# Two attention layers mixed by a gate: the last turns of a P @ V unit take their blocks from a table

## The chip, the cores and the metric

The kernel runs on one core of a Trainium2 chip. The metric is the device time of one execution in microseconds (us), as the median of several runs. A profiled execution is a run of its own, with its own time.

## The reference

Two attention layers read the same x (2048 tokens of 512 features, 32 heads of 16). Layer A is plain softmax attention over all 2048 keys. Layer B works in four segments of 512 tokens: causal softmax attention inside a segment, mixed by a learned gate per head with a linear memory of the segments before. The results are mixed by a gate per token.

```python
# A
p = softmax(einsum("bhqd,bhkd->bhqk", q, k) * scale); o = einsum("bhqk,bhkd->bhqd", p, v)
a = o.reshape(B, S, D) @ wo
# B, for each of 4 segments s
p = softmax(einsum(qs, ks) * scale + mask); a_dot = p @ vs
a_mem = (phi(qs) @ M) / (phi(qs) @ z + 1e-6)
o = g * a_mem + (1 - g) * a_dot;  M += phi(ks).T @ vs;  z += sum(phi(ks))
# together
g = sigmoid((x * gate_w).sum(-1)); return g * a + (1 - g) * b
```

## The kernel before

Everything is fp32 or split into two parts that together carry it. The first stage (to about 330 us) projects q, k and v of both layers to DRAM. The second stage, which this change touches, is a software pipeline in *slots*; the Python loop that writes the program decides its whole order, and every engine then follows its own list in that order.

A **unit** is one side (A or B), one group of four heads and one chunk of 512 queries. There are 32 units of each side, taken in turn, A and then B; only the last pair stands the other way round. An A unit has 64 slots, one for each head and block of 128 keys; a B unit has 10, since its mask leaves out blocks. So a pair of units has 74 slots. In each slot:

- `score_part` (L662): TensorE makes one score product `st` of 128 keys by 512 queries (L677), and ScalarE takes its exponential into a tile `p` (L697, L700). There are three PSUM banks for `st`.
- `max_part` (L213), for the slot 96 places further on: TensorE makes the product `sm` of 128 queries by 512 keys (L204), and VectorE reduces it to row maxima `pm` (L225 for A; for B L237, which also applies the causal mask, in pieces). There are four PSUM banks for `sm`, L605. The maxima are later put into q so that the scores come out with them subtracted.

The two products of a slot use different rows of the array, and the trace shows them start within some nanoseconds of each other.

After each third slot there is a **turn** (L948 on). In a turn, `some_values` (L712) takes ready *blocks* from `queue` and multiplies them with v into one PSUM bank `ops` (L733). A block is 128 keys of four heads for A; B's ten blocks are the pieces in `PIECES` (L709): four of one key block, three of the next, then one, then two. Neighbouring blocks that share v are done by one **run** of matmuls, up to four blocks wide; a run is 4 heads x 2 records in the trace, whatever its width (a group in the timeline named x8 is one run, x16 two). A turn ends with its unit: `some_values` returns when a unit's last block is done, ScalarE copies `ops` out (`oraw`, L737), and for most A units 12 matmuls of the output projection of an earlier chunk (`output`, L838) take the next three turns, four matmuls in each; no blocks are done in those turns.

How many blocks a turn may take is `MOST = 3`, or one more when `jam` says that the queue is long. For B, `left` is zero, so that one more is allowed whenever over six blocks wait:

```python
def jam(n):
    left = SLOTS["A"] - queue[0][2] if queue and queue[0][1][0] == "A" else 0
    return 64 * (len(queue) - LOW) > (HIGH - LOW) * left
```

In the last 96 slots (`wide`) there are no more maxima, and turns of up to eight blocks come every six slots; after the last slot likewise.

Of the kernel before, what the change touches and what calls it, by code (L numbers as in the profile page):

```python
# [32 lines left out]
SLOTS = {"A": 64, "B": 10}  # L33
# [3 lines left out]
MOST = 3  # L37
LOW, HIGH = 6, 14
# [8 lines left out]
def gated_mix(ctx, tc, x, xT, wqkv, a_wo, b_wq, b_wk, b_wv, b_wo, beta, gate_w, out):  # L47
# [61 lines left out]
    nS = len(slots)  # L109
# [103 lines left out]
    def max_part(m, bank):  # L213

        u, (r, i) = maxs[m]
        side, g, c = u
        if u not in pmt:
            pmt[u] = mp.tile([128, 4, 4] + [4] * (side == "A"), F32, tag="pm" + side, name="pm")
        pm = pmt[u]
        ps = bank()  # L220
        if side == "A":

            kc, s, h = i // 8, i % 8 // 2, 2 * r + i % 2
            max_product(ps, u, h, s, 0, CH, kt_[u, kc])
            nc.vector.tensor_reduce(pm[:, h, s, kc:kc + 1], ps, axis=AX.X, op=ALU.max)  # L225
            flush_rows()
        else:


            k = kt_[u, c]  # L230
            mine = [(2 * r + h, s, 128 * (s == 2) + 256 * (s == 1 and h), 128 * (s + 1))
                    for h, s in (((0, 0), (0, 2)), ((0, 1), (1, 1)), ((1, 0), (1, 2)), ((0, 3),), ((1, 3),))[i]]
            for h, s, n0, w in mine:
                max_product(ps, u, h, s, n0, w, k)
            flush_rows()
            for h, s, n0, w in mine:
                rows_left.append(lambda h=h, s=s, n0=n0, w=w: nc.vector.tensor_tensor_reduce(  # L237
                    out=tri["rest"][:, 0:w], in0=ps[:, n0:n0 + w], in1=tri["mask"][:, CH - w:], scale=-1.0, scalar=3.0e38,
                    op0=ALU.add, op1=ALU.min, accum_out=pm[:, h, s:s + 1]))
            rows_left.pop(0)()  # L240
        if m == last_max[u]:
            def finish():

                due = min(e for e in a_last if e >= last_max[u]) + LATE_T
                late.append((min(due, first[u] + LEAD - 12), u, finish_max(u)))
            todo.append((m + 1, finish))

    def run_todo(m):

        for e in [e for e in todo if e[0] <= m]:  # L250
            todo.remove(e)
            e[1]()

    def run_late(pool, tag, m):
        while us := [e for e in late if e[0] < m][:2]:
            for e in us:
                late.remove(e)
            transpose_max(us, pool, tag)
# [3 lines left out]
    def loads(m):  # L262

        m = min(m, len(maxs) - 1)
        while loaded[0] <= m:
            u, (r, i) = maxs[loaded[0]]
            if loaded[0] == first_max[u]:
                load_q(u)
            kc = u[2] if u[0] == "B" else i // 8
            if (u, kc) not in kt_:  # L270
                load_k(u, kc)
            loaded[0] += 1
# [384 lines left out]
    wide = range(nS - LEAD + 2, nS - 4)  # L657
    assert wide.start % (2 * BURST) == wide.stop % (2 * BURST) == 0

    queue = []  # L660
# [51 lines left out]
    def some_values(n, most):  # L712

        while queue and most and queue[0][0] <= n:
            _, u, i = queue.pop(0)
            most -= 1
            side, g, c = u
            w = 1
            while (queue and most and queue[0][0] <= n and queue[0][1] == u and (i + w) // 4 == i // 4
                   and (side == "A" or PIECES[i + w][0] == PIECES[i][0])):  # L720
                queue.pop(0)
                most -= 1
                w += 1
            p = pt_[u, i // 4]
            if side == "A":
                c0 = q0 = 128 * (i % 4)
                v = vt[u][:, i // 16, i // 4 % 4]
            else:
                b, c0, q0 = PIECES[i]
                v = vt[u][:, b]  # L730
            done = i + w == SLOTS[side]
            for h in range(4):
                nc.tensor.matmul(ops[32 * h:32 * h + 17, q0:q0 + 128 * w], v[:, 17 * h:17 * h + 17], p[:, h, c0:c0 + 128 * w],  # L733
                                 start=(i == 0), stop=done, tile_position=(0, 32 * h))
            if done:
                raw = ob.tile([128, CH], F32, tag="o", name="oraw")
                nc.scalar.copy(raw, ops)  # L737
                nc.sync.dma_start(od[side, c][4 * g:4 * g + 4].rearrange("h r t -> (h r) t"), raw)
                stored.add(u)
                if side == "B" and c and g % 2 == 0:  # L740
                    octet("M", g // 2, c, n + 4)
                if (side, g ^ 1, c) in stored and u != ("A", NG - 1, NCH - 1):
                    octet(side, g // 2, c, n + (20 if side == "B" and (g < 5 or c < last) else 8))
                if u in between:
                    shared.extend(output(*between[u]))
                return
# [113 lines left out]
    def output(c, b, pairs, then, ps=ops):  # L860

        ks = [(os, o, i) for os in pairs for o in os for i in range(2)]
        for k in ks:
            def f(n, k=k):
                os, o, i = k
                assert loaded_blocks[c, b, os] > len(blocks) - 2
                t = blocks[loaded_blocks[c, b, os] - 1][:, i, o % 2].unsqueeze(1)
                list(products(ps, t, 0, "AB"[i], o, k == ks[0], k == ks[-1]))[n]()
                if k == ks[-1] and n == 2:
                    then(ps, c, b)  # L870
            for n in range(3):
                yield lambda n=n, f=f: f(n)
# [54 lines left out]
    for (side, o), b in early + [(k, b) for k in closing[:-1] for b in range(4) if (k, b) not in early]:  # L927
        close(nS - 66 if ((side, o), b) in early else max(nS, end[side, 2 * o + 1, last] + 60), side, o, b)

    def jam(n):  # L930


        left = SLOTS["A"] - queue[0][2] if queue and queue[0][1][0] == "A" else 0
        return 64 * (len(queue) - LOW) > (HIGH - LOW) * left

    filled = [0]
    n = 0
    while n < nS or queue or beside or filled[0] < len(fill):
        for f in beside.pop(n, []):
            f()  # L940
        if n < nS:
            score_part(n)
        m = n + LEAD
        if m < nS:
            loads(m + PRE)

            max_part(m, lambda: banks[m % 4])
        run_todo(m)  # L948
        if n >= nS or n % (2 * BURST if n in wide else BURST) == (2 * BURST if n in wide else BURST) - 1:
            if shared:  # L950
                for _ in range(4):
                    shared.pop(0)()
            else:
                some_values(n, 8 if n >= nS or n in wide else MOST + jam(n))
            if n < 5:


                for i in range(4):
                    nc.tensor.matmul(ops[:, 128 * i:128 * i + 128], identf, identf, start=True, stop=True)
            if any(e[0] < m + 1 for e in late):  # L960
                run_late(st_ps, "st", m + 1)
            else:
                for _ in range(0 if n >= nS and queue else 4):
                    if filled[0] == len(fill) or fill[filled[0]][0] > n:
                        break
                    fill[filled[0]][1]()
                    filled[0] += 1
        n += 1
# [12 lines left out]
def build():  # L981
    import concourse.bacc as bacc
    nc = bacc.Bacc("TRN2", target_bir_lowering=False, num_devices=1)
    shapes = {"x": (S, D), "xT": (D, S), "wqkv": (D, 3 * D), "a_wo": (D, D), "b_wq": (D, D), "b_wk": (D, D),
              "b_wv": (D, D), "b_wo": (D, D), "beta": (H,), "gate_w": (D,)}
    args = [nc.dram_tensor(n, s, F32, kind="ExternalInput").ap() for n, s in shapes.items()]
    out = nc.dram_tensor("out", (S, D), F32, kind="ExternalOutput").ap()
    with tile.TileContext(nc) as tc:
        gated_mix(tc, *args, out)
    return nc  # L990
# [23 lines left out]
```

## Time and profile before

| | |
|---|---|
| median of 3 runs | 1809.33 us (1809.08 to 1810.16) |
| the profiled execution: its own time | 1810.57 us |
| its span | 1808.7 us |
| TensorE matmul busy in the span | 1795.2 us (99%) |
| VectorE busy | 1574.9 us (87%) |
| ScalarE busy | 1447.0 us (80%) |
| GpSimd busy | 604.2 us (33%) |
| granted TensorE clock | 1.00 throughout |

The span begins with the program's first instruction and ends with its last; the profiled execution's own time has 1.9 us around it. Busy TensorE time is modelled by the profile, with the ends of pipelined matmuls overlapping, so that 99% does not say that TensorE has no room.

### The profile page before, as it was taken

The page shows a single profiled execution, that of the slowest core. Times are in us where ns is not written, and L with a number is a line of the kernel's source. Part 1 is how long each engine was busy: PE and PEld are TensorE (multiplying, and loading weights), DVE is VectorE, ACT ScalarE, POOL GpSimd, SP SyncE. Part 2 cuts the span into 40 slices and gives each one's busy share as a digit, 9 for nine tenths or more (in the row PEclk, how much of TensorE's full clock was granted, in tenths as well). Part 3 has the DMA queues.
Part 4 walks back from the last instruction along what each step waited for, and adds up shares of the span by engine and source line. Part 5 has one row for each costly group of instructions (what it writes and reads, how often), then busy time and mean ns, then how long its engine had stood idle before and what let it go on. Part 6 is the DMA issues. An engine that isn't in the chain of part 4 may idle for free.

```text
span 1808.7 us, 41561 instructions
## 1 busy us (share of the span) xinstructions
PE 1795.2 (99%) x15409; PEld 943.9 (52%) x15409; DVE 1574.9 (87%) x3333; ACT 1447.0 (80%) x2766; POOL 604.2 (33%) x708
## 2 busy tenths in 40 slices
PE   9999999999999999999999999999999999999998
PEld 7887766544444444444444444444444444444444
DVE  4224677899999999999999999999999999999920
ACT  5445444788888888888888888888888888888894
POOL 3001222234141414343433434342534342525442
PEclk9999999999999999999999999999999999999999
DMA  6568645543434344545454545454544443444541
GB/s 222 199 221 267 218 166 178 167 125 109 119 109 119 109 119 121 143 126 144 126 143 126 142 124 143 125 145 111 143 125 142 122 141 120 143 123 128 155 146 61
DMA packets 140617, 258.46 MB, mean 143 GB/s; under 512 B 36184, under 2 KB 60280, under 8 KB 139904
## 3 DMA queue, kind: packets, MB, share of 16 engines
q1 hardware_dynamic: 138912, 254.15, 47.1%
q8 instruction: 123, 2.02, 0.5%
q0 software_dynamic: 1216, 1.14, 0.2%
q14 instruction: 78, 0.64, 0.1%
q10 hardware_dynamic: 288, 0.52, 0.1%
HBM read 171.25 MB, written 83.25 MB: 141 GB/s over the span
## 4 chain that ended last, share of the span: by engine, by line
PE 90%; DVE 3%; ACT 3%; DMA 2%; issue 1%; POOL 1%; SPq 0%; POOLq 0%; DVEq 0%; ACTq 0%
PE ops L733 32%; PE st L677 27%; PE sm L204 14%; PE pr L313 10%; PE ops L838 4%; DVE pm L225 2%; PE sm L838 2%; ACT p L700 1%; DMA raw<-xT 1%; POOL mn L373 1%; PE num L495 1%; DMA vs<-wqkv 1%; DMA qdB<-q 0%; DMA qdA<-q 0%; ACT full L368 0%
## 5 line engine op out<-in xcount | busy, mean ns | idle before, releaser
L700 ACT ACTIVATE p<-st 128x512 f32<-128x512 f32 x2261 | 1190.2, 602 | 155.9 <-PE sm L204 96.0
L225 DVE TENSOR_REDUCE pm<-sm 128x1 f32<-128x512 f32 x2048 | 1280.2, 683 | 12.7 <-PE sm L204 11.6
L204 PE MATMUL sm<-kA,qA 48*128 48x512 f32 x2048 | 678.0, 435 | 0.3 <-DVE pm L237 0.2
L677 PE MATMUL st<-qA,kA 50*128 50x512 f32 x2014 | 670.4, 433 | 0.8 <-ACT p L697 0.5
L733 PE MATMUL ops<-p,vA 128*17 128x384 f32 (+3 forms) x7376 | 559.5, 406 | 0.0
L677 PEld LDWEIGHTS st<-qA,kA 50*128 50x128 f32 x2014 | 329.9, 185 | 391.7 <-ACT p L700 345.4
L204 PEld LDWEIGHTS sm<-kA,qA 48*128 48x128 f32 x2048 | 328.4, 184 | 22.1 <-issue 7.1
L792 POOL TENSOR_TENSOR rcp<-rec,minus 128x32 f32<-128x32 f32 x43 | 234.3, 5448 | 119.2 <-DMA rec<-dend 82.8
L733 PEld LDWEIGHTS ops<-p,vA 128*17 128x17 f32 x7376 | 152.4, 96 | 220.8 <-issue 178.6
L237 DVE CUSTOM_DVE_ANT_0 rest<-sm,mask 128x128 f32<-128x128 f32 (+3 forms) x512 | 247.0, 482 | 2.4 <-PE sm L204 1.5
L681 POOL TENSOR_SCALAR_AFFINE_SELECT p<-p 128x512 f32<-128x512 f32 x128 | 79.5, 639 | 351.2 <-ACT p L700 337.9
L204 PE MATMUL sm<-kB,qB 48*128 48x128 f32 (+3 forms) x512 | 166.2, 385 | 0.0
L376 DVE TENSOR_TENSOR q<-full,q 128x512 fp32r<-128x512 f32 x64 | 44.4, 694 | 87.3 <-ACT q L369 87.2
L677 PE MATMUL st<-qB,kB 50*128 50x512 f32 (+1 forms) x495 | 115.7, 333 | 1.7 <-ACT p L700 1.4
L677 PEld LDWEIGHTS st<-qB,kB 50*128 50x128 f32 x495 | 72.4, 186 | 59.5 <-ACT p L700 51.7
L733 PE MATMUL ops<-p,vB 128*17 128x512 f32 (+3 forms) x1024 | 87.2, 437 | 0.1
L204 PEld LDWEIGHTS sm<-kB,qB 48*128 48x128 f32 x512 | 79.9, 184 | 0.0
L368 ACT COPY full<-pr 128x512 f32<-128x512 f32 x64 | 37.4, 584 | 51.1 <-PE pr L313 50.9
L373 POOL TENSOR_SCALAR mn<-full 128x512 f32<-128x512 f32 x24 | 35.8, 1490 | 101.7 <-ACT full L368 81.3
L186 POOL CAST ms<-pm 128x16 fp32r<-128x16 f32 x32 | 6.3, 198 | 175.3 <-DVE pm L237 175.3
L186 POOL CAST ms<-nm 128x16 fp32r<-128x16 f32 x32 | 6.7, 210 | 172.8 <-DVE nm L182 172.8
L313 PE MATMUL pr<-xh,wql 128*128 128x512 f32 x128 | 54.8, 428 | 1.0 <-ACT xh L426 0.7
(178 smaller groups left out, 1580.6 us busy)
## 6 DMA issues: line engine op xcount, KB each, us to landing
kA<-kdA SPq DMA_DIRECT2D x256, 128.0 KB
vA<-vdA SPq DMA_DIRECT2D x31, 544.0 KB
kA<-kdA SPq DMA_DIRECT2D x256, 64.0 KB
qdA<-q SPq DMA_DIRECT2D x32, 256.0 KB
kdA<-q SPq DMA_DIRECT2D x32, 256.0 KB
qdB<-q SPq DMA_DIRECT2D x32, 256.0 KB
qA<-qdA SPq DMA_DIRECT2D x64, 128.0 KB
kdB<-q SPq DMA_DIRECT2D x32, 256.0 KB
```

The lines of the kernel that those rows point to most:

```text
L204: nc.tensor.matmul(ps[:, n0:n0 + n], rows(qt[u][:, :, s * 128:(s + 1) * 128], h, 48), rows(k[:, :, k0:k0 + n], h, 48), start=True, stop=True)
L225: nc.vector.tensor_reduce(pm[:, h, s, kc:kc + 1], ps, axis=AX.X, op=ALU.max)
L237: rows_left.append(lambda h=h, s=s, n0=n0, w=w: nc.vector.tensor_tensor_reduce(out=tri["rest"][:, 0:w], in0=ps[:, n0:n0 + w], in1=tri["mas ...
L313: nc.tensor.matmul(ps, l(a, k), r(b, k), start=(n == 0), stop=(n == 11))
L373: nc.gpsimd.tensor_scalar_min(ph["mn"], full, 0.0)
L376: nc.vector.tensor_sub(q2, full, q1.bitcast(F32))
L677: nc.tensor.matmul(ps[:, n0:n0 + CH - q0], rows(k[:, :, b * 128:(b + 1) * 128], h, 50), rows(q[:, :, q0:], h, 50), start=True, stop=True)
L681: nc.gpsimd.affine_select(out=x, in_=x, pattern=[[0, 4], [1, 128]], base=0, channel_multiplier=-1, compare_op=ALU.is_ge, fill=0.0)
L700: nc.scalar.activation(p[:, h], ps, AF.Exp, scale=SCALE)
L733: nc.tensor.matmul(ops[32 * h:32 * h + 17, q0:q0 + 128 * w], v[:, 17 * h:17 * h + 17], p[:, h, c0:c0 + 128 * w], start=(i == 0), stop=done ...
L792: eng.tensor_tensor(r, rec, minus, op=ALU.pow)
L838: yield lambda i=i, x=x, w=w: nc.tensor.matmul(ps, t[:, b, x], wos[side][:, o, w], start=start and i == 0, stop=stop and i == 2)
```

## The change

Which number of blocks a turn takes is no longer three plus `jam`. A table by side gives it for certain numbers of blocks that are left of the unit at the head of the queue; where the table has no entry, the old rule holds.

```diff
-    def jam(n):
-        left = SLOTS["A"] - queue[0][2] if queue and queue[0][1][0] == "A" else 0
-        return 64 * (len(queue) - LOW) > (HIGH - LOW) * left
+    ends = {"A": {9: 3, 8: 4, 7: 3, 6: 3, 5: 5}, "B": {10: 3, 7: 3, 4: 4}}
+
+    def most():
+        if not queue:
+            return 0
+        side = queue[0][1][0]
+        left = SLOTS[side] - queue[0][2]
+        over = 64 * (len(queue) - LOW) > (HIGH - LOW) * (left if side == "A" else 0)
+        return ends[side].get(left, MOST + over)
...
-                some_values(n, 8 if n >= nS or n in wide else MOST + jam(n))
+                some_values(n, 8 if n >= nS or n in wide else most())
```

## The prediction

> **What bounds the kernel now.** I began with the page's busy times, then asked for the busy time of each engine in stretches of the long second stage, then for the groups of instructions kept apart by shape.
>
> ```profile
> span 1808.7 us, 41561 instructions
> ...
> PE 1795.2 (99%) x15409; PEld 943.9 (52%) x15409; DVE 1574.9 (87%) x3333; ACT 1447.0 (80%) x2766; POOL 604.2 (33%) x708
> ...
> 400.00:700.00 300.00, 298.38 (x2948) 143.35 (x2942) 300.00 (x653) 264.93 (x514) 89.15 (x111) 1.00 0.38 110
> 700.00:1000.00 300.00, 300.00 (x2892) 140.95 (x2890) 299.00 (x635) 264.52 (x511) 115.25 (x132) 1.00 0.48 134
> ...
> L733 PEld LDWEIGHTS ops<-p,vA 128*17 128x17 f32 x7376 | 152.4, 96 | 220.8 <-issue 178.6
> L838 PE MATMUL ops<-woA,blk 128*128 128x512 f32 x132 | 46.0, 430 | 0.0
> ```
>
> In a row of a stretch the second figure is TensorE's busy time, the fourth VectorE's. Both look full, and only one can be the bound. From 400 to 700 us VectorE has not a hundredth of idle time; from 700 on, where output projections are worked in between units (132 matmuls of this kind at 6 a unit make 22 such units), it loses 1.0 us in 300. So in this stage the row maxima set the pace, and what a change of TensorE's turns can win is what VectorE still loses to TensorE. Idle time as the page counts it misses most of that, since a reduction of 0.68 us overlaps its follower. So I read VectorE's timeline at three neighbouring B units, all after an output projection.
>
> ```profile
> 877.93 4.34 DVE L225 TENSOR_REDUCE pm<-sm 128x1 f32<-128x512 f32 x7
> 882.19 0.68 DVE L237 CUSTOM_DVE_ANT_0 rest<-sm,mask 128x512 f32<-128x512 f32 x1
> ...
> 884.60 4.89 DVE L225 TENSOR_REDUCE pm<-sm 128x1 f32<-128x512 f32 x8
> 889.50 0.69 DVE L237 CUSTOM_DVE_ANT_0 rest<-sm,mask 128x512 f32<-128x512 f32 x1
> ```
> ```profile
> 922.22 4.48 DVE L225 TENSOR_REDUCE pm<-sm 128x1 f32<-128x512 f32 x7
> 926.70 0.69 DVE L237 CUSTOM_DVE_ANT_0 rest<-sm,mask 128x512 f32<-128x512 f32 x1
> ...
> 929.12 4.88 DVE L225 TENSOR_REDUCE pm<-sm 128x1 f32<-128x512 f32 x8
> 933.92 0.68 DVE L237 CUSTOM_DVE_ANT_0 rest<-sm,mask 128x512 f32<-128x512 f32 x1
> ```
> ```profile
> 831.02 4.48 DVE L225 TENSOR_REDUCE pm<-sm 128x1 f32<-128x512 f32 x7
> 835.50 0.69 DVE L237 CUSTOM_DVE_ANT_0 rest<-sm,mask 128x512 f32<-128x512 f32 x1
> ...
> 837.32 0.68 DVE L237 CUSTOM_DVE_ANT_0 rest<-sm,mask 128x512 f32<-128x512 f32 x1
> ...
> 837.93 5.00 DVE L225 TENSOR_REDUCE pm<-sm 128x1 f32<-128x512 f32 x8
> 842.85 0.68 DVE L237 CUSTOM_DVE_ANT_0 rest<-sm,mask 128x512 f32<-128x512 f32 x1
> ```
>
> Take the distance from a row's start to the next row's, by the number of reductions. The undisturbed price is the second pair of the second fence: 933.92 - 929.12 = 4.80 for 8, so 0.60 each. Against that the seven at 831.02 lose 4.48 - 4.20 = 0.28, those at 922.22 0.28, those at 877.93 0.06; the eight at 837.93 lose 4.92 - 4.80 = 0.12, those at 884.60 0.10. Since a pair of units is 74 slots, two more than 24 turns, the position of a unit against the turns repeats with every third pair: I take these three as the three kinds, seven of each, with one unit left over near the end of the stage.
>
> TensorE's timeline around the third kind says why:
>
> ```profile
> 831.16 0.50 PE L677 MATMUL st<-qA,kA 50*128 50x512 f32 x1
> ...
> 832.06 1.05 PE L733 MATMUL ops<-p,vB 128*17 128x512 f32 x8
> 833.04 0.50 PE L677 MATMUL st<-qA,kA 50*128 50x512 f32 x1
> ...
> 833.95 1.06 PE L733 MATMUL ops<-p,vB 128*17 128x384 f32 x16
> ...
> 834.94 0.50 PE L204 MATMUL sm<-kB,qB 48*128 48x512 f32 x1
> ...
> 835.84 0.62 PE L733 MATMUL ops<-p,vB 128*17 128x256 f32 x8
> ...
> 836.40 0.50 PE L204 MATMUL sm<-kB,qB 48*128 48x512 f32 x1
> ...
> 837.57 1.05 PE L733 MATMUL ops<-p,vA 128*17 128x512 f32 x8
> 838.56 0.49 PE L677 MATMUL st<-qA,kA 50*128 50x512 f32 x1
> ...
> 839.49 1.05 PE L733 MATMUL ops<-p,vA 128*17 128x512 f32 x8
> 840.47 0.50 PE L677 MATMUL st<-qA,kA 50*128 50x512 f32 x1
> ...
> 841.37 0.84 PE L733 MATMUL ops<-p,vA 128*17 128x384 f32 x8
> ...
> 842.15 0.50 PE L204 MATMUL sm<-kB,qB 48*128 48x512 f32 x1
> ```
>
> A turn lasts from its row to the next product: four blocks 832.06 to 833.04, 0.98; three blocks 841.37 to 842.15, 0.78; two blocks 835.84 to 836.40, 0.56. So a block is 0.21. A cycle (three products, one turn) takes 833.04 - 831.16 = 1.88 and 834.94 - 833.04 = 1.90 with four blocks, against 3 x 0.60 = 1.80 of VectorE: each turn of four in a row is 0.08 to 0.11 too long. How much VectorE has in stock is the time from a product's start to its own work on it: 835.50 - 834.94 = 0.56 is the shortest (the product itself is 0.50), 837.32 - 836.40 = 0.92 after the turn of two, so a stock of 0.36, and 842.85 - 842.15 = 0.70, a stock of 0.14.
>
> **The change part by part.** The built program's order of instructions shows what the table does. For A, nearly nothing: apart from the first unit, A's turns are as before, since `jam` makes the numbers left miss the table, and many A units still end with one block. For B, the turns of the ten blocks go from 4, 4 (a run of 3 and one of 1), 2 to 3, 3 (1 and 2), 4 (1, 1 and 2) wherever the queue holds them all, in the 22 units after output projections among others. They remain three turns, so each later turn, copy and DMA keeps its place in its queue (SP's, ScalarE's and GpSimd's lists have the same instructions in the same order), and the blocks are as many. The last 96 slots don't change.
>
> What is added is two more runs in a unit. A run's own price: 4 blocks in one run took 0.98 at 832.06, 3 and 1 took 834.94 - 833.95 = 0.99. So at most 0.01 a run, 0.02 a unit; I count it in.
>
> What moves: two times 0.21 leaves the first two turns, and 0.42 comes to the third. Stock of the third kind, step by step. At the product of 831.16 it is nil, since of the 0.28 lost from 831.02 on only 0.07 and 0.10 belong to the two cycles behind it, and the rest fell before. First turn of three: the cycle is 1.88 - 0.21 = 1.67, stock 0.13. Second: 1.90 - 0.21 + 0.01 = 1.70, stock 0.23. Both stalls are gone: the two cycles lost 0.07 and 0.10, 0.17 in all. Third turn, four blocks: 836.40 - 834.94 + 0.42 + 0.01 = 1.89, against VectorE's 837.32 - 835.50 = 1.82: stock 0.16. Before, the turn of two made a stock of 0.36 here; so that stock is lower, and the A turns that follow are the question.
>
> There a second effect answers. After the turn of two, the next cycle took 838.56 - 836.40 = 2.16, of which 837.57 - 836.40 = 1.17 went to the products instead of 833.95 - 833.04 = 0.91. These rows tell why, and what a closing turn of four does:
>
> ```profile
> 836.92 0.60 ACT L737 COPY oraw<-ops 128x512 f32<-128x512 f32 x1
> ```
> ```profile
> 868.79 1.05 PE L733 MATMUL ops<-p,vA 128*17 128x512 f32 x8
> ...
> 870.73 0.97 PE L838 MATMUL ops<-woA,blk 128*128 128x512 f32 x3
> ```
> ```profile
> 869.91 0.59 ACT L737 COPY oraw<-ops 128x512 f32<-128x512 f32 x1 [0.24 <-PE ops L733]
> ```
>
> The copy of `ops` ends at 837.52, and the next turn, which writes that bank, starts at 837.57: TensorE waited for it, 1.17 - 0.91 = 0.26. After a closing turn of four (an A unit's) the copy ends at 870.50, still ahead of the next user at 870.73, though it starts 1.12 after its turn does. That user came 870.73 - 868.79 = 1.94 after the turn's start, against 0.98 + 0.91 = 1.89 without any wait. So the copy is hidden by the longer turn and the products behind it, and the cycle is 0.91 to 0.96 + 0.98 = 1.89 to 1.94 instead of 2.16; if that cover failed, it would be the 0.26 again. Stock: 0.16 + 1.81 - 1.89 to 1.94 = 0.03 to 0.08, no stall. (VectorE's 1.81 is 837.93 - 837.32 plus two reductions.) The next turn of four: 1.80 - (840.47 - 838.56) = -0.11, so a stall of 0.03 to 0.08, I take 0.04, where 0.12 was. The third kind wins 0.17 + 0.08 = 0.25.
>
> First kind: 0.06 in B's turns, and the 0.10 at 884.60, for in its cycles the copy is hidden likewise:
>
> ```profile
> 882.46 0.84 PE L733 MATMUL ops<-p,vA 128*17 128x384 f32 x8
> 884.36 0.84 PE L733 MATMUL ops<-p,vA 128*17 128x128 f32 x16
> 886.05 1.06 PE L733 MATMUL ops<-p,vA 128*17 128x256 f32 x16
> ```
>
> Two turns of three, 1.90 and 1.69: the first holds 0.21 of ScalarE catching up with the copy, and a stock of 0.10 or more is left from it. Together 0.16. Second kind: 0.17 in B's turns as in the third; behind them it loses nothing before (the 4.80), and the stock of 0.03 to 0.08 lasts, as a turn of three follows. So three units win 0.25 + 0.16 + 0.17 = 0.58, seven times that is 4.1 us, and for the 22nd I count nothing. The ten other B units lie where VectorE loses nothing (400 to 700, and before), or in the last 96 slots: nothing. The span goes from 1808.7 to 1804.6. The profiled execution, 1810.57, is 1.2 above the median; from the median, 1809.33 - 4.1 = **1805.2 us**.
>
> A rule that speaks against the change: the Trainium skill, page "TensorE: Matmul & The Clock Gate", section "Wait — 56ns, not 53.3ns?", gives some 62 ns of sequencer time for each matmul where hardware decoding is off, which bounds short ones. By that the new third turn with its three runs, 24 records, would take 1.49 us as an estimate. The trace disagrees: the 16 records at 884.36 lie within 0.84 us, where the rule asks for 0.99.
>
> **The rivals.** *Short runs wait for weights.* Two runs of one block in a row stand nowhere in this program so far. The row of weight loads gives 96 ns each; were the four loads of a pass of one block done one after another and not hidden, the pass would take 0.38 instead of 0.10, a run with its two passes 0.56 more, the second turn 0.56 and the third 1.12 more. Less a stock of some 0.2 that is 1.5 us a unit, over 22 units +33, less the 4: 1838 us. It makes the kernel slower than now from some 0.4 a unit on. Against it: the turn of 1 and 2 at 884.36 has the 0.84 of the single run at 882.46. 5%. The rule of the Trainium skill that is weighed above would act in the same place, and milder.
>
> *The closing turn gives it back.* If the stock after the turn of four is nil, A's stalls of 0.12 and 0.10 stay and only B's go: 0.06 + 0.17 + 0.17 = 0.40, seven times 2.8, 1806.5 us. For it: my margin there is 0.03 to 0.08. 20%.
>
> *The copy is not hidden.* If the next cycle still takes 2.16, the stock there falls to 0.16 + 1.81 - 2.16 = -0.19: the second and third kind lose what they won, only the first gains, some 0.1: 1808.6 us. For it: ScalarE is busy 264.5 of 300 us from 700 on, and the copy stands in one list with the exponentials. Against it: 869.91. 10%.
>
> *More than forecast.* Every stall behind B's turns goes: 0.16 + 0.17 + 0.29 = 0.62, and some 0.2 for the 22nd: 1804.8 us; that lies inside the forecast's spread.
>
> **How the numbers follow.** The forecast has 65%. The range goes from 1804.2 (all stalls gone, and 0.6 of scatter, about half of what lies between the lowest and the highest of the three runs) to 1808.6 (the copy). What a measurement can tell from no change is about 0.2%, 3.6 us. Faster by more than that: most of the forecast (50 of 65) and a little of the second rival, 54%. Within it: the rest of the forecast, most of the second rival and the third, 41%. Slower by more: 5%.
>
> **What would show it.** In the changed profile, VectorE's rows behind the output projections run at 0.60 a reduction through B's three turns; the closing turn of four is 0.98 to 1.00 long; the next turn starts 1.9 after it and not after the copy; VectorE's busy time from 700 to 1000 us rises from 299.0 towards 299.5, and its last reductions come some 4 us earlier. I am wrong if B's third turn is over 1.2 long, if the stalls of 0.1 in the A turns behind it have grown, or if the next turn starts with the copy's end.

## The result, and the profile after

| | before | after |
|---|---|---|
| median of 13 runs | 1810.37 us | 1805.54 us |
| lowest to highest | 1808.81 to 1811.05 | 1803.96 to 1808.43 |
| span of the profiled execution | 1808.7 | 1804.1 |
| VectorE's first to last reduction of an A unit | 1537.5 | 1533.6 |

The ratio is 0.9977, with a 95% interval of 0.9968 to 0.9985: 2.7 to 5.8 us faster, where 4.1 were forecast. (It is taken over all the runs and is not that of the two medians, which would be 0.9973.) The last line of the table is the cleanest measure, since it leaves out the first 190 us and what their length differs by from one execution to the next. It comes from these rows, of the kernel before and after; the two times ahead of the semicolon are the first and the last start:

```profile
L225 DVE TENSOR_REDUCE pm<-sm x2048: 669/681/697, 192.1 to 1729.6; 128x1 f32<-128x512 f32 x187
```
```profile
L225 DVE TENSOR_REDUCE pm<-sm x2048: 669/679/694, 191.4 to 1725.0; 128x1 f32<-128x512 f32 x187
```

So 3.9 us were won between VectorE's first and last reduction, and 0.7 of the span's 4.6 had come before, in work that the change doesn't touch. I call this length VectorE's stretch below; each kernel's is from the same row of its own trace.

VectorE's timeline after, at units of the first, second and third kind:

```profile
876.51 4.27 DVE L225 TENSOR_REDUCE pm<-sm 128x1 f32<-128x512 f32 x7
880.70 0.68 DVE L237 CUSTOM_DVE_ANT_0 rest<-sm,mask 128x512 f32<-128x512 f32 x1
...
883.11 4.87 DVE L225 TENSOR_REDUCE pm<-sm 128x1 f32<-128x512 f32 x8
887.90 0.68 DVE L237 CUSTOM_DVE_ANT_0 rest<-sm,mask 128x512 f32<-128x512 f32 x1
```
```profile
920.59 4.38 DVE L225 TENSOR_REDUCE pm<-sm 128x1 f32<-128x512 f32 x7
924.89 0.68 DVE L237 CUSTOM_DVE_ANT_0 rest<-sm,mask 128x512 f32<-128x512 f32 x1
...
927.30 4.93 DVE L225 TENSOR_REDUCE pm<-sm 128x1 f32<-128x512 f32 x8
932.15 0.68 DVE L237 CUSTOM_DVE_ANT_0 rest<-sm,mask 128x512 f32<-128x512 f32 x1
```
```profile
829.77 4.39 DVE L225 TENSOR_REDUCE pm<-sm 128x1 f32<-128x512 f32 x7
834.08 0.68 DVE L237 CUSTOM_DVE_ANT_0 rest<-sm,mask 128x512 f32<-128x512 f32 x1
...
835.89 0.68 DVE L237 CUSTOM_DVE_ANT_0 rest<-sm,mask 128x512 f32<-128x512 f32 x1
...
836.50 5.03 DVE L225 TENSOR_REDUCE pm<-sm 128x1 f32<-128x512 f32 x8
841.44 0.68 DVE L237 CUSTOM_DVE_ANT_0 rest<-sm,mask 128x512 f32<-128x512 f32 x1
```

Read as before, at 0.60 a reduction: the seven lose 0 (880.70 - 876.51 = 4.19), 0.10 and 0.11, where they lost 0.06, 0.28 and 0.28; the eight lose 0, 0.05 and 0.14, where they lost 0.10, 0 and 0.12. B's turns gave what was forecast. What was to be seen behind them came true in the first kind and not in the third. The same stretch on TensorE, third kind:

```profile
829.91 0.50 PE L677 MATMUL st<-qA,kA 50*128 50x512 f32 x1
...
830.81 0.84 PE L733 MATMUL ops<-p,vB 128*17 128x384 f32 x8
831.58 0.52 PE L677 MATMUL st<-qA,kA 50*128 50x512 f32 x1
...
832.62 0.84 PE L733 MATMUL ops<-p,vB 128*17 128x128 f32 x16
...
833.40 0.50 PE L204 MATMUL sm<-kB,qB 48*128 48x512 f32 x1
...
834.30 1.06 PE L733 MATMUL ops<-p,vB 128*17 128x128 f32 x24
...
835.29 0.49 PE L204 MATMUL sm<-kB,qB 48*128 48x512 f32 x1
...
836.20 1.05 PE L733 MATMUL ops<-p,vA 128*17 128x512 f32 x8
837.18 0.50 PE L677 MATMUL st<-qA,kA 50*128 50x512 f32 x1
```

and on ScalarE:

```profile
830.08 0.59 ACT L878 COPY part<-ops 128x512 f32<-128x512 f32 x1
830.56 3.15 ACT L700 ACTIVATE p<-st 128x512 f32<-128x512 f32 x6
...
835.43 0.59 ACT L737 COPY oraw<-ops 128x512 f32<-128x512 f32 x1
```

B's turns are 0.77 (830.81 to 831.58), 0.78 and 0.99 long. The cycles, product to product, are 1.67, 1.82, 1.89 and 1.89. The copy of the finished unit ends at 836.02 and the next turn starts at 836.20: hidden. Of my cycles one is wrong, the second, forecast at 1.70. In it the products take 832.62 - 831.58 = 1.04 instead of 0.91. ScalarE says why: it had copied the output projection's result (`keep`, `part`) just before, and then ran six exponentials without a pause; TensorE's third score product of that cycle had to wait for a bank that was still being read. The weight load of that product shows the wait, and what ended it:

```profile
832.19 0.18 PEld L677 LDWEIGHTS st<-qA,kA 50*128 50x128 f32 x1 [0.30 <-ACT p L700]
```

The sign that I had named for the busy time hardly shows. VectorE is busy for 299.19 us from 700 to 1000, against 299.00 before and 299.5 looked for:

```profile
700.00:1000.00 300.00, 300.00 (x3006) 144.03 (x2995) 299.19 (x637) 265.75 (x514) 116.87 (x134) 1.00 0.50 133
```

What was won stands in the distances between starts, and only to a small part in the idle time.

### The profile page after: what moved, and what is told of

It reads as the page before. It is cut to its first block, busy times and chain, and to the rows that moved or that the text cites. A ratio compares the mean times of both kernels' runs of the same rounds, so it can differ in the third digit from the quotient of the medians.

```text
span 1804.1 us, 42457 instructions
## 1 busy us (share of the span) xinstructions
PE 1791.4 (99%) x15857; PEld 954.9 (53%) x15857; DVE 1571.3 (87%) x3333; ACT 1449.2 (80%) x2766; POOL 604.0 (33%) x708
## 4 chain that ended last, share of the span: by engine, by line
PE 91%; DVE 2%; ACT 2%; DMA 2%; POOL 1%; issue 1%; SPq 0%; POOLq 0%; ACTq 0%; DVEq 0%
PE ops L733 32%; PE st L677 27%; PE sm L204 14%; PE pr L313 10%; PE ops L838 4%; PE sm L838 2%; DVE pm L225 1%; ACT p L700 1%; POOL mn L373 1%; DMA raw<-xT 1%; PE num L495 1%; DMA qdA<-q 0%; DMA vs<-wqkv 0%; DMA qdB<-q 0%; DVE q L376 0%
## 5 line engine op out<-in xcount | busy, mean ns | idle before, releaser
L733 PE MATMUL ops<-p,vA 128*17 128x128 f32 (+3 forms) x7368 | 559.7, 407 | 0.0
L733 PEld LDWEIGHTS ops<-p,vA 128*17 128x17 f32 x7368 | 152.3, 96 | 223.7 <-issue 179.5
L733 PE MATMUL ops<-p,vB 128*17 128x128 f32 (+3 forms) x1480 | 88.1, 353 | 0.1
```

## The experiments

VectorE's stretch is 1537.5 before and 1533.6 after. Ratios are of a kernel's runs to those of the kernel before, with their intervals; they can't tell most of these kernels apart, the stretch and the rows can. Besides, I compared the 2048 starts of VectorE's reductions one by one with those of the kernel before, each counted from its own first: that tells where along the stretch time is won. A pair of units is taken from one B unit to the next, and a mean by kind is over the seven units of that kind.

**A's entries alone.**

```diff
-    ends = {"A": {9: 3, 8: 4, 7: 3, 6: 3, 5: 5}, "B": {10: 3, 7: 3, 4: 4}}
+    ends = {"A": {9: 3, 8: 4, 7: 3, 6: 3, 5: 5}, "B": {}}
```

> The table keeps its entries for A and loses those for B, so that B's turns are 4, 4, 2 again. Theory (the stock of row maxima that VectorE has in front of it decides, and only B's turns change it): the kernel before, within 0.5 us, and the losses of 0.28 and 0.12 in VectorE's rows around B's turns are back. Rival (A's entries bring a part): between the two kernels, 1 us or more faster than before.

Ratio 0.9998 (0.9988 to 1.0007); the stretch is 192.9 to 1730.4, 1537.5, as before, and pair by pair the starts agree with the kernel before within 0.06 us. So two executions of nearly the same order repeat that closely, and the whole effect is B's.

**Every run one block wide.**

```diff
-            while (queue and most and ...
+            while (False and queue and most and ...
```

> The changed kernel with every run of P @ V one block wide: turns and their sizes are as they are, 2368 runs instead of 1105. Theory (a run's own price is 0.005 to 0.01 us, since its weights are loaded behind the matmuls before it): turns of three and four get 0.01 to 0.03 longer, VectorE loses that where its stock is nil, 0 to 3 us slower than the changed kernel. Rival 1 (weights are not hidden: 0.56 a run): several hundred us slower. Rival 2 (sequencer time of 62 ns a matmul, the rule of the Trainium skill's page TensorE: Matmul & The Clock Gate as I used it): a turn of three takes 1.49 us, some 300 us slower.

Ratio 0.9995 (0.9985 to 1.0004); the stretch is 190.8 to 1725.9, 1535.1, so 1.5 more than the changed kernel for 1262 more runs (18944 matmul records on L733 against 8848, eight a run; the expectation's count is one higher). By the ratios it would be 3.3 more, with intervals that touch. All of the 1.5 comes behind the first output projection, at 733 us; ahead of it, where VectorE has stock, these runs cost nothing. A turn of three single runs, here the first row, x24, to the product behind it, takes 840.31 - 839.53 = 0.78, as with one run:

```profile
839.53 0.85 PE L733 MATMUL ops<-p,vA 128*17 128x128 f32 x24
840.31 0.50 PE L204 MATMUL sm<-kB,qB 48*128 48x512 f32 x1
```

Short runs are nearly free here; both rivals fall. By the rule of the Trainium skill's page "TensorE: Matmul & The Clock Gate" (section "Wait — 56ns, not 53.3ns?"), as I used it, 24 matmuls would have asked for 1.49 us, an estimate; the trace has 0.78. The page gives that rule for hardware decoding switched off, and no run here says which it was: the trace shows that this bound does not act here, not that the page is wrong.

**The other order in B: 4, 2, 4.**

```diff
+    ends = {"A": {}, "B": {10: 4, 6: 2, 4: 4}}
```

> B's turns are 4, 2, 4; nothing else differs from the changed kernel but A's entries of the table, which do nothing. Theory (the order inside the unit matters by the stock at each turn): the first turn loses its 0.07 again in the second and third kind, the turn of two fills the stock, the closing turn of four hides the copy, A's turns behind lose at most what they lose in the changed kernel: 2 to 3 us faster than before over the second stage. Rival 1 (all that matters is that the closing turn hides the copy): as the changed kernel, 3.9. Rival 2 (all that matters is that no two turns of four stand together inside B): 1.5 or less.

Ratio 0.9991 (0.9982 to 1.0000); the stretch is 190.8 to 1727.5, 1536.7: 0.8 less than before. But in this execution the granted clock fell once, at 423 to 427 us, well ahead of the first output projection. The row of that stretch (granted clock is the figure 0.77; VectorE is busy 4.61 of 6.00) and its neighbours:

```profile
400.00:424.00 24.00, 23.81 (x214) 11.10 (x206) 24.00 (x59) 21.17 (x42) 6.12 (x9) 0.99 0.16 47
424.00:430.00 6.00, 6.00 (x64) 2.79 (x64) 4.61 (x10) 4.34 (x9) 5.07 (x5) 0.77 0.46 139
430.00:460.00 30.00, 30.00 (x325) 14.82 (x323) 30.00 (x63) 26.41 (x52) 10.70 (x13) 1.00 0.44 120
```

VectorE is idle for 1.39 there, and its starts come 1.46 later from there on. Without that the stretch is 2.2 less than before: within the theory's 2 to 3, well off 3.9 and above 1.5. By kind the pairs win 0.19, 0.04 and 0.07, where the changed kernel wins 0.19, 0.17 and 0.17. So both the order inside B and the closing turn count.

**The closing copy cut short, in the kernel before.** Twice, since the first try had a flaw of its own:

```diff
 # first try
+                if side == "B":
+                    nc.gpsimd.memset(raw[:, 64:], 1.0)
+                    nc.scalar.copy(raw[:, :64], ops[:, :64])
...
 # second try: two fixed tiles, set once at the start
...
+                raw = oraws[len(stored) % 2]
+                cut = 64 if side == "B" else CH
+                nc.scalar.copy(raw[:, :cut], ops[:, :cut])
```

> The kernel before, but ScalarE's copy of a finished B unit takes 64 of 512 columns; the rest is set to one. Theory (after a closing turn of two TensorE waits 0.26 for that copy, and the losses of 0.12 and 0.10 in the A turns behind it come from that wait): the cycle behind it falls from 2.16 to 1.9, those losses go, the 0.17 in B's own turns stay; about 1.5 us faster than before. Rival (the A turns lose time because turns of four follow each other, whatever the copy does): before within 0.3 us.

The first try was slower, 1.0026 (1.0015 to 1.0037), stretch 190.3 to 1733.1, 5.3 longer. TensorE's list of waits has a row that stands in none of the others:

```profile
PE mt_ps L195 <- POOL ms L187: 4.6, 6, 1.2
```

TensorE waited six times, 4.6 us, for the maxima that GpSimd prepares for their transpose; the added memset stood in GpSimd's list. At the first of these waits it ran only at 791.74, behind a long division, so the unit was stored late; GpSimd's next division, which reads that unit back, started 20.4 us after the one before it instead of 17.3, and the maxima came behind that. Read for the question asked, this run is spoilt by its own edit.

> The kernel before once more with a short copy of a finished B unit (64 of 512 columns; the rest of the stored tile is old), this time without setting the rest on GpSimd in each unit: two fixed tiles are set once at the start. Theory: as the rows of the earlier attempt have it inside the units, where the A turns behind B lost 0.05 and nothing instead of 0.12 and 0.10, and B's own 0.17 stayed: about 1.1 us faster than before over the second stage, and no loss of 1 us anywhere. Rival (the short copy itself makes the kernel slower, as it came out then): 3 us or more slower than before.

The second try: 0.9992 (0.9983 to 1.0001), stretch 192.7 to 1728.4, 1535.7, so 1.8 shorter, where 1.1 was expected. VectorE's rows at a unit of the third kind:

```profile
831.21 4.47 DVE L225 TENSOR_REDUCE pm<-sm 128x1 f32<-128x512 f32 x7
835.69 0.69 DVE L237 CUSTOM_DVE_ANT_0 rest<-sm,mask 128x512 f32<-128x512 f32 x1
...
838.11 4.92 DVE L225 TENSOR_REDUCE pm<-sm 128x1 f32<-128x512 f32 x8
842.95 0.68 DVE L237 CUSTOM_DVE_ANT_0 rest<-sm,mask 128x512 f32<-128x512 f32 x1
```

The seven still lose 4.48 - 4.20 = 0.28, the eight 0.04 instead of 0.12. By kind the pairs win 0.13, 0.01 and 0.07. B's turns are as they were and A's loss goes with the copy alone: the two terms of the forecast are two effects, and this is the second by itself. Both rivals fall, that the short copy makes the kernel slower and that A's turns lose time whatever the copy does. Of the 0.7 beyond the 1.1 expected, 0.1 comes ahead of the first output projection and 0.1 in the 22nd pair, neither of which was counted, and the rest in the pairs, most of it in the first kind.

**The output projection's copy cut short, in the changed kernel.**

```diff
-        nc.scalar.copy(part[b], ps)
+        nc.gpsimd.memset(part[b][:, 64:], 0.0)
+        nc.scalar.copy(part[b][:, :64], ps[:, :64])
 # and the same in leave
```

> The changed kernel, but ScalarE's copies of the output projection's result (keep and leave) take 64 of 512 columns; the rest of the result is set to zero. In the changed profile the first of B's turns is followed by a cycle of 1.75 to 1.82 us instead of the 1.67 that I forecast, since the exponentials start late behind that copy. Theory (TensorE waits there for ScalarE, and that is why the third kind of unit still loses 0.05 and 0.09 in A's first turns): the cycle falls to about 1.68, those losses fall to 0.04 or less, 0.7 to 1.2 us faster than the changed kernel. Rival (the first cycle is long for another reason, or its stock would be lost anyway): the changed kernel within 0.3 us.

```profile
836.18 4.89 DVE L225 TENSOR_REDUCE pm<-sm 128x1 f32<-128x512 f32 x8
840.99 0.68 DVE L237 CUSTOM_DVE_ANT_0 rest<-sm,mask 128x512 f32<-128x512 f32 x1
```
```profile
830.51 0.84 PE L733 MATMUL ops<-p,vB 128*17 128x384 f32 x8
832.20 0.84 PE L733 MATMUL ops<-p,vB 128*17 128x128 f32 x16
```

B's first turn starts 1.69 before the second, where the changed kernel has 832.62 - 830.81 = 1.81, and the eight lose 4.81 - 4.80 = 0.01 instead of 0.14. Ratio 0.9976 (0.9965 to 0.9987); the stretch is 189.9 to 1723.8, 1533.9, 0.3 longer than the changed kernel's; but here too the granted clock fell once, to 0.57 from 374 to 378 us, and VectorE's starts come 1.2 later from there on. Behind it the kernel is 0.9 faster, which the theory gave, and the third kind wins most of that: 0.27 a pair instead of 0.17. So the misjudged cycle was ScalarE's doing.

**VectorE's work cut.** Row maxima over 448 of 512 columns.

```diff
-            nc.vector.tensor_reduce(pm[:, h, s, kc:kc + 1], ps, axis=AX.X, op=ALU.max)
+            nc.vector.tensor_reduce(pm[:, h, s, kc:kc + 1], ps[:, :448], axis=AX.X, op=ALU.max)
```

> The changed kernel, but VectorE's row maxima of A take 448 of 512 columns. Theory (VectorE sets the pace of the second stage and TensorE is close behind, with cycles of 1.68, 1.89 and 2.07 us): the pace passes to TensorE, 35 to 60 us faster, and VectorE no longer busy throughout; not the 64 x 0.067 = 4.3 us a pair, 120 us in all, that VectorE alone would give. Rival (TensorE sets the pace already): 5 us or less.

Ratio 0.9864 (0.9851 to 0.9878); the stretch is 191.2 to 1702.2, 1511.0: 22.6 shorter than the changed kernel's. That VectorE sets the pace holds. My 35 to 60 was too much: TensorE stands closer behind than I had added up, above all where the change acts. Of the 22.6, 15.3 are won by 733 us; behind the first output projection 7.3 are left, 0.34 a pair, though each pair's 64 reductions were made some 4 us shorter (0.615 instead of 0.679 each). From there on TensorE's products, which VectorE waits for, come hardly faster than VectorE had worked. As an estimate from this, some 7 us is all that an order of turns without a stall could still win there. Now it is VectorE that waits:

```profile
700.00:1000.00 300.00, 300.00 (x3004) 144.98 (x3001) 282.38 (x648) 268.22 (x518) 118.14 (x136) 1.00 0.46 130
```

**Two attempts at more.** What VectorE still loses lies mostly in the three turns of the output projection. In one kernel its matmuls take four turns of three (with one more buffer for `p`), in the other A's turns of four are spread:

```diff
 # four turns of three
-NP = 6
+NP = 7
-                for _ in range(4):
+                for _ in range(3):
 # A's turns spread, in most()
+        over = over and (prior[0] < 2 or len(queue) > 16)   # prior: turns of four just before
```

> The changed kernel with the twelve matmuls of an output projection in four turns of three instead of three turns of four, and one more buffer for p, since blocks wait longer. Most of what VectorE still loses (0.25 to 0.66 us a pair) lies in those three turns, whose cycles are 2.03 to 2.08 us. Theory (a cycle of 2.07 falls to about 1.86 and the stock holds): the losses there fall by two thirds, some 6 us; one turn fewer for blocks makes up to three more turns of four in a pair, which give back 0 to 5 us: 1 to 6 us faster than the changed kernel. Rival (what is taken from these turns comes back in full in the turns that catch up): within 1 us of it, or slower.

> The changed kernel, with the output projection in three turns of four as there, and A's turns of four spread: a turn of four may not follow two others while at most sixteen blocks wait. In the built program no three turns of four stand together any more in A's part of the stage shown. Theory (stock): the losses of the changed kernel in A's turns behind B (0.05 and 0.09 in the second and third kind) and further on go, those in the projection's turns (0.25 to 0.66 a pair) stay or fall where the turns ahead of them leave more stock: 1 to 2 us faster than the changed kernel (3.9 faster than before over the second stage). Rival: within 0.5 us.

Four turns of three: 0.9977 (0.9968 to 0.9986), stretch 191.2 to 1723.4, 1532.2. A's turns spread: 0.9975 (0.9965 to 0.9985), stretch 190.6 to 1723.0, 1532.4. Both are 1.2 to 1.4 shorter than the changed kernel's 1533.6, at the lower end of what was expected, and by their medians (1805.51 and 1805.32) not to be told from it. For the first, most of what the projection's turns no longer lose is lost again in the turns that catch up: against the changed kernel, three pairs win 1.3 in the first ten reductions from the projection on and lose 1.2 of it over the rest. What the seventh buffer does by itself was not run. Both together, with fours allowed early:

```diff
-LOW, HIGH = 6, 14
+LOW, HIGH = 0, 1
... # NP and the projection's turns of three as above
+        over = over and (prior[0] < 2 or len(queue) > 12)
```

> The output projection's matmuls again in four turns of three with seven buffers for p; besides, a turn of four may not follow two others while at most twelve blocks wait (LOW, HIGH = 0, 1, so that fours come early). Theory (with the projection's turns cut, what is left is lost where three and more turns of four stand together, and a turn of three gives 0.11 to the stock each time): 1 to 3 us faster over the second stage than the run with four turns of three alone (5.3 faster than before). Rival (fewer fours in a row here are more fours elsewhere, and the loss only moves): within 0.7 us of that run.

A miss: 1.0023 (1.0011 to 1.0036), stretch 190.2 to 1729.8, 2.1 longer than before. It loses already where no other order did (two executions lost there to their clock), ahead of the first output projection. From 335 to 700 us, this kernel first and the changed one below:

```profile
335.00:700.00 365.00, 362.30 (x3390) 158.43 (x3394) 364.59 (x794) 316.63 (x621) 105.81 (x136) 1.00 0.39 113
```
```profile
335.00:700.00 365.00, 362.67 (x3684) 176.19 (x3680) 365.00 (x799) 322.85 (x625) 106.03 (x136) 1.00 0.40 115
```

By its built order the turns there go 4, 4, 3, 4, 4, 3, 2, 4, 3, 4, 1, 3 and so on: fours come early, and turns of one and two follow them. As I read it, these short turns come when the stock can take no more; no run shows that by itself. I had only thought of fours standing together. The rows show 0.4 of idle time and five operations fewer; by the starts, this kernel is 3.2 us behind the kernel before when the first output projection comes. Behind that point it wins 1.2, where four turns of three alone win 5.1. So its early fours cost 3.2, and its later turns give up 3.9 more of what it was to win. Part of its ratio is something else again: see the granted clock below.

## Why the prediction was right, and where it wasn't

- *VectorE sets the pace, and the change is worth what VectorE stops losing*: shown, by the run with lighter reductions and by the rows; but from 733 us on even the lighter reductions shorten a pair by only 0.34 us, so there TensorE stands close behind.
- *A's entries do nothing*: shown.
- *A run costs at most 0.01*: held; the turn of 1, 1 and 2 is 0.99 long, and 1262 more runs cost 1.5 us of the stretch in all.
- *B's own turns win 0.06, 0.17 and 0.17*: the rows have 0.06, 0.18 and 0.17.
- *The closing turn of four hides the copy*: held, at 836.02 against 836.20; the copy's part by itself is shown by the second try with the short copy.
- *The turns of A behind B*: the step that failed is the stock of 0.23 after B's second turn. That cycle was 1.82, not 1.70, since ScalarE came late from the projection's copy. The stock was 834.08 - 833.40 - 0.56 = 0.12; then 835.89 - 835.29 - 0.56 = 0.04 instead of 0.16; then the two turns of four lose 0.14 in the third kind instead of 0.04, and 0.05 in the second instead of nothing. The turn of two before had paid for that copy without my seeing it, in a stock that it filled in any case. One of my own signs of being wrong, that the stalls in A's turns have grown, thus came true by a little: 0.12 to 0.14 in the third kind, 0 to 0.05 in the second.
- In sum the units shown win 0.16, 0.13 and 0.15, 0.44 for three, against 0.58. Not all units of a kind are alike: comparing the starts of VectorE's reductions one by one, and taking the mean over the seven, the kinds win 0.19, 0.17 and 0.17, 0.53. So the term of the third kind, 0.25, was the one too large. Seven times 0.53 is 3.7; the 22nd pair, counted as nothing, wins 0.1, and another 0.1 comes ahead of the first projection. The stretch has 3.9: the forecast's 4.1 is off by a twentieth. That the medians differ by 4.8 is more than VectorE's stretch explains; the interval, 2.7 to 5.8, holds both.
- *1805.2 us*: that the median of 1805.54 lies so near is in part luck. The forecast started from 1809.33, the median of three runs; that of thirteen is 1810.37, 1.0 higher, and the medians fell by 0.7 more than forecast.

The rivals: short runs that wait for weights, and a copy that isn't hidden, are refuted. That the closing turn gives everything back came true in part: in the third kind A's loss of 0.12 is 0.14 now, in the first it is gone.

## What to carry to other kernels

Where one engine sets the pace and another feeds it through a few buffers, what counts is not the feeder's total but the order of its long and short pieces: a long piece is free while there is stock and costs its whole excess where there is none, and a short piece wins nothing when the stock is full. Ahead of the first projection, where VectorE has stock, the change won 0.1 in 540 us. Look for stalls that the idle column doesn't show, by the distance between starts over a long row, and add up the stock piece by piece. A third engine that shares the feeder's buffers, here ScalarE with its copies, belongs in that sum: one copy there moved the stock by 0.1.

## What I hadn't expected of the hardware

The granted clock fell for a few microseconds in single executions, while TensorE was busy throughout. The means of 0.57 and 0.77 above are both one fall to half clock for 3.4 us, at a cost of 1.2 us with the short copy of the projection and 1.5 us with 4, 2, 4:

```profile
374.30:377.70 3.40, 3.40 (x27) 1.53 (x23) 3.03 (x10) 2.08 (x4) 3.24 (x5) 0.50 0.41 125
```
```profile
423.40:426.80 3.40, 3.40 (x31) 1.65 (x32) 2.16 (x4) 1.94 (x4) 3.40 (x1) 0.50 0.48 140
```

Both times it was in the first units of the second stage; no run here shows why. The mean clocks of all the runs suggest that it is not rare: of the changed kernel's thirteen runs the two at 0.998 took 1808.3 and 1807.6, and the ten at 1.000 have a median of 1805.5. (One at 0.999 took 1808.4, so it is not the clock alone.) Of the twelve runs of the last kernel above, four turns of three with early fours, three stood at 0.994 and took 1818 to 1820 us. Its four at 1.000 have a median of 1810.2, against 1809.2 for the eleven at 1.000 of the kernel before that were run with it; so much of its 1.0023 is the clock's.

The first reduction of an A unit starts between 189.9 and 192.9 us in these executions, though the first stage has the same instructions in all of them but for what the edits set at the start. So up to 3 us of what single runs differ by is there before the part under study begins.
